# A gated feed-forward kernel on one core: first half of x first, DMA transposes for the second half, small first weight groups, warm-up matmuls and a split last tile

## The chip, the cores and the metric

The kernel runs on one core of a Trainium2 chip. The metric is device time in microseconds (us) of one execution. The kernel before takes 311.3 us (median of 12 runs, 311.04 to 311.73). The span of the profile is shorter than the device time: by 1.7 us in every run of the kernel before, by 1.9 to 2.2 us in every run of the changed kernel and its edits. So spans are compared with spans and times with times, and spans show about 0.35 us more of a gain than times do.

## The reference

```python
B, S, D, F = 32, 32, 1024, 3584          # 1024 tokens, bf16 everywhere
def reference(x, w_gate, w_up, w_down):
    return (gelu(x @ w_gate) * (x @ w_up)) @ w_down   # gelu: tanh approximation
```

In tiles of 128: 8 token tiles (`tt`), 8 chunks of D (`dc`), 28 chunks of F (`ft`). Matmuls take 512 tokens at a time, so there are two halves of the tokens (`th` = 0 and 1). Stage 1 has 28 x 2 = 56 "jobs" of 8 gate and 8 up matmuls. Stage 2 has 16 output pieces of 28 matmuls. That is 1,344 matmuls of 512 columns.

## The kernel before

Stage 1 needs x transposed (`xT`, with D on the partitions). The kernel loads all of x, transposes it on TensorE into PSUM, and VectorE copies it to SBUF. Only then does job 0 start.

```python
# SP: loads                                   (cut)
for (t0, t1) in x_chunks:                     # two DMAs of 1 MB
    sp.dma_start(out=x_nat[:, t0:t1, :], in_=x_v[:, t0:t1, :]).then_inc(sem_x, 16)
for fg in range(NFG):                         # 7 groups of 4 ft, 1 MB each, two buffers
    ... w_gate group, w_up group, then one chunk of w_down ...
for j2, (tt, dh) in enumerate(jobs2):         # stores: one row of tiles (256 KB) each
    if dh == DH - 1: ...

# TensorE                                     (cut)
pe.wait_ge(sem_x, 16 * NX)                    # ALL of x
for tt in range(TT):
    for dc in range(DT):
        ins = pe.transpose(...)               # 64 transposes
    ins.then_inc(sem_tp, 1)
pe.wait_ge(sem_xT, TT)                        # ALL copies
for j, (fg, ftl, th) in enumerate(jobs1):     # th is the fastest index
    ... 8 gate matmuls, 8 up matmuls ...
for j2, (tt, dh) in enumerate(jobs2):
    ... 28 matmuls of 512 columns ...

# VectorE: copies of xT, then the elementwise work of stage 1
# ScalarE: activations of stage 1, then all 16 evictions of stage 2
```

## Time and profile before

| | before |
|---|---|
| device time, median | 311.3 us |
| span of the profile | 310.0 us |
| TensorE busy | 294.9 us (95%) |
| first matmul of job 0 | 16.65 us |
| last eviction starts | 306.94 us |

The profile page's summary of the chain of work that ended last in the kernel before; shares of the span, by engine and by line:

```profile
PE 95%; DMA 3%; issue 1%; DVE 1%; ACT 0%; SPq 0%
PE ps L213 62%; PE ps L234 31%; DMA x_nat<-in_x_dram 3%; PE ps L193 2%; DVE xT L248 1%; ACT o_sb L310 0%; SPq L122 0%
```

L213 is stage 1 and L234 is stage 2, both on TensorE. The rest of the chain is the load of x, its transposes (L193) and its copies (L248), all at the start, and one eviction (L310) at the end. So time can come only from the two ends, or from shorter matmuls.

The timeline of the kernel before, its first 25 us. Columns: start in us, duration in us, engine, line, operation, output and inputs, count; in brackets the idle time before and what ended it. PE is TensorE and PEld its weight loads, DVE is VectorE, ACT is ScalarE, and SPq is SP, the engine that issues the DMAs. The traces hold 16 landing records for each DMA (32 for the two loads of x here); a load counts as landed at the last of them.

```profile
0.80 0.99 SPq L122 DMA_DIRECT2D x_nat<-in_x_dram  x2
...
9.39 6.20 PE L193 MATMUL ps<-ident,x_nat 128*128 128x128 bf16 x64 [9.39 <-DMA x_nat<-in_x_dram]
...
14.71 1.89 DVE L248 COPY xT<-ps 128x1024 bf16<-128x1024 bf16 x3 [0.16 <-PE ps L193]
16.65 1.41 PEld L213 LDWEIGHTS ps<-xT,wg_sb 128*128 128x128 bf16 x8 [1.23 <-DVE xT L248]
16.88 1.67 PE L213 MATMUL ps<-xT,wg_sb 128*128 128x512 bf16 x7 [1.28 <-DVE xT L248]
```

TensorE waits 9.4 us for x, transposes for 6.2 us, and waits for the last copy. The record of the very first matmul is missing (x7, not x8), so the first weight load, 16.65 us, is read as its start; the 1.28 us in the last line count to the second matmul. One transpose every 107 ns becomes one every 56 ns at 14.6 us: the clock of TensorE rose there. Below, "cold" is the slow pace and "warm" the fast one; for 512 columns they are 427 and 216 ns.

The timeline of the kernel before, its last us:

```profile
306.94 0.60 ACT L310 ACTIVATE o_sb<-ps 128x512 bf16<-128x512 f32 x1 [5.45 <-PE ps L234]
307.56 0.33 SPq L154 DMA_DIRECT2D out_dram<-o_sb  x1
```

The stores of the kernel before in its list of DMAs: count, size of one, median us from issue to landing.

```profile
out_dram<-o_sb SPq DMA_DIRECT2D x8, 256.0 KB, 2.0
```

After the last matmul come an eviction of 0.60 us, a store of 256 KB that lands 2.00 us after its issue, and 0.4 us to the end of the span.

### The profile page before, as it was taken

The numbers are of one execution on the slowest core, as the hardware profiler recorded it, in microseconds if no ns is written. First come the engines' busy times: TensorE is split into PE (matmuls) and PEld (weight loads), VectorE is DVE, ScalarE is ACT, GpSimd is POOL, SyncE is SP. The second block draws the span as 40 slices with busy tenths as digits, with TensorE's granted clock in tenths as the row PEclk, the third lists the DMA queues.
The fourth block names the chain that finished last, engine by engine and source line by source line (L and its number), as shares of the span: only waits on it lengthen the run. The fifth ranks groups of instructions, "written<-read, shape, count | busy, mean of one in ns | idle before, by whom it ended". The sixth has DMA issues, their size and how long they took to land.

```text
span 310.0 us, 3408 instructions
## 1 busy us (share of the span) xinstructions
PE 294.9 (95%) x1381; PEld 137.5 (44%) x1408; DVE 136.3 (44%) x120; ACT 102.1 (33%) x186; POOL 71.7 (23%) x62
## 2 busy tenths in 40 slices
PE   0789999999999999999999999999999999999995
PEld 0734444444444444444444444444444444444442
DVE  0534677667776777667766776674000000000000
ACT  1016544454445444554455445543000100100010
POOL 0003334333433343334333433343000000000000
PEclk9999999999999999999999999999999999999999
DMA  6990009005600910480097000000000000000000
GB/s 244 355 346 5 0 17 367 24 1 176 233 0 0 336 72 0 129 279 0 1 284 261 0 2 0 0 0 2 34 0 36 2 32 34 2 34 34 2 34 34
DMA packets 20479, 26.43 MB, mean 85 GB/s; under 512 B 496, under 2 KB 14832, under 8 KB 20464
## 3 DMA queue, kind: packets, MB, share of 16 engines
q1 hardware_dynamic: 20464, 26.22, 25.2%
q8 instruction: 11, 0.18, 0.2%
q14 instruction: 4, 0.03, 0.0%
HBM read 24.12 MB, written 2.10 MB: 85 GB/s over the span
## 4 chain that ended last, share of the span: by engine, by line
PE 95%; DMA 3%; issue 1%; DVE 1%; ACT 0%; SPq 0%
PE ps L213 62%; PE ps L234 31%; DMA x_nat<-in_x_dram 3%; PE ps L193 2%; DVE xT L248 1%; ACT o_sb L310 0%; SPq L122 0%
## 5 line engine op out<-in xcount | busy, mean ns | idle before, releaser
L213 PE MATMUL ps<-xT,wg_sb 128*128 128x512 bf16 x438 | 104.8, 379 | 1.8 <-DVE xT L248 1.3
L213 PE MATMUL ps<-xT,wu_sb 128*128 128x512 bf16 x440 | 105.1, 379 | 0.4
L178 POOL TENSOR_TENSOR hT<-gu_sb,s_sb 128x512 bf16<-128x512 f32 x56 | 71.0, 1267 | 143.4 <-ACT s_sb L294 143.4
L264 DVE SCALAR_TENSOR_TENSOR z_sb<-g_sb 128x512 f32<-128x512 f32 x56 | 97.1, 1733 | 0.0
L234 PE MATMUL ps<-wd_sb,hT 128*128 128x512 bf16 x439 | 96.4, 379 | 0.5
L282 ACT ACTIVATE g_sb<-ps 128x512 f32<-128x512 f32 x56 | 33.4, 597 | 119.1 <-PE ps L213 119.1
L259 DVE TENSOR_TENSOR gu_sb<-g_sb,ps 128x512 f32<-128x512 f32 x56 | 38.5, 688 | 66.2 <-ACT g_sb L285 66.2
L213 PEld LDWEIGHTS ps<-xT,wg_sb 128*128 128x128 bf16 x448 | 43.7, 98 | 53.9 <-DVE xT L248 1.2
L234 PEld LDWEIGHTS ps<-wd_sb,hT 128*128 128x128 bf16 x448 | 43.9, 98 | 52.8
L213 PEld LDWEIGHTS ps<-xT,wu_sb 128*128 128x128 bf16 x448 | 43.8, 98 | 52.9
L310 ACT ACTIVATE o_sb<-ps 128x512 bf16<-128x512 f32 x16 | 9.6, 597 | 83.6 <-PE ps L234 83.6
L294 ACT ACTIVATE s_sb<-z_sb 128x512 f32<-128x512 f32 x56 | 35.4, 632 | 1.9 <-DVE z_sb L264 1.9
L285 ACT ACTIVATE g_sb<-ps 128x512 f32<-128x512 f32 x56 | 33.1, 591 | 0.0
L193 PE MATMUL ps<-ident,x_nat 128*128 128x128 bf16 x64 | 6.2, 289 | 9.4 <-DMA x_nat<-in_x_dram 9.4
L248 DVE COPY xT<-ps 128x1024 bf16<-128x1024 bf16 x8 | 5.3, 689 | 11.2 <-PE ps L193 11.2
L193 PEld LDWEIGHTS ps<-ident,x_nat 128*128 128x128 bf16 x64 | 6.1, 135 | 9.4 <-issue 9.4
L282 ACT ACT_TABLE_LOAD x1 | 1.3, 1283 | 0.8 <-PEq L328 0.8
L294 ACT ACT_TABLE_LOAD x1 | 1.3, 1283 | 0.0
L165 POOL TENSOR_SCALAR_AFFINE_SELECT ident<-ones 128x128 bf16<-128x128 bf16 x1 | 0.3, 294 | 0.1
L163 POOL MEMSET ones<- 128x128 bf16 x1 | 0.2, 205 | 0.3 <-POOLq L328 0.3
L328 POOL MEMSET const-float32-0.0<- 128x1 f32 x1 | 0.1, 99 | 0.3 <-issue 0.3
L328 POOL MEMSET const-bfloat16-1.0<- 128x1 bf16 x1 | 0.1, 102 | 0.0
(2 smaller groups left out, 0.2 us busy)
## 6 DMA issues: line engine op xcount, KB each, us to landing
wg_sb<-in_w_gate_dram SPq DMA_DIRECT2D x7, 1024.0 KB, 6.7
wu_sb<-in_w_up_dram SPq DMA_DIRECT2D x7, 1024.0 KB, 9.3
wd_sb<-in_w_down_dram SPq DMA_DIRECT2D x7, 1024.0 KB, 11.3
x_nat<-in_x_dram SPq DMA_DIRECT2D x2, 1024.0 KB, 6.8
out_dram<-o_sb SPq DMA_DIRECT2D x8, 256.0 KB, 2.0
```

What stands on the lines that cost most here:

```text
L165: pool.affine_select(out=ident[:], in_=ones_sb[:], pattern=[[1, P]], compare_op=ALU.is_equal, fill=0.0, base=0, channel_multiplier=-1,).th ...
L178: pool.tensor_tensor(out=hT[:, ft, th * TW : (th + 1) * TW], in0=gu_sb[:, k, :], in1=s_sb[:, k, :], op=ALU.mult,).then_inc(sem_h, 1)
L193: ins = pe.transpose(out=bank_bf[:, dc * P : (dc + 1) * P], in_=x_nat[:, tt, dc * P : (dc + 1) * P], identity=ident[:],)
L213: last = pe.matmul(bank, lhsT=wsb[:, slot, dc, ftl * P : (ftl + 1) * P], rhs=xT[:, dc, th * TW : (th + 1) * TW], start=(dc == 0), stop=(dc ...
L234: last = pe.matmul(bank, lhsT=hT[:, fc, tt * P : (tt + 1) * P], rhs=wd_sb[:, fc, dh * DW : (dh + 1) * DW], start=(fc == 0), stop=(fc == FT ...
L248: dve.tensor_copy(out=xT[:, :, tt * P : (tt + 1) * P], in_=bank_bf[:, 0 : DT * P].rearrange("p (dc t) -> p dc t", dc=DT),).then_inc(sem_xT, 1)
L259: dve.tensor_tensor(out=gu_sb[:, k, :], in0=g_sb[:, k, :], in1=bu, op=ALU.mult).then_inc(sem_d1, 1)
L264: dve.scalar_tensor_tensor(out=z_sb[:, k, :], in0=g2_sb[:, k, :], scalar=GELU_A, in1=g_sb[:, k, :], op0=ALU.add, op1=ALU.mult,).then_inc(s ...
L282: act.activation(out=g_sb[:, k, :], in_=bg, func=ACT.Copy).then_inc(sem_a1, 1)
L285: act.activation(out=g2_sb[:, k, :], in_=bg, func=ACT.Square).then_inc(sem_a1, 1)
L294: act.activation(out=s_sb[:, k, :], in_=z_sb[:, k, :], func=ACT.Sigmoid, scale=GELU_C2).then_inc(sem_a2, 1)
L310: act.activation(out=o_sb[:, ob, dh * DW : (dh + 1) * DW], in_=ps[:, s2, 0:DW], func=ACT.Copy,).then_inc(sem_o, 1)
```

## The change

Its intent is to start stage 1 sooner and end sooner:

1. Only the first half of x (two DMAs of 512 KB) is loaded and transposed on TensorE. The second half goes from HBM straight into `xT` by eight DMA transposes, issued behind the first three weight groups.
2. The first jobs are reordered, so that 7 jobs need only the first half of the tokens.
3. The first two weight groups hold 2 x 128 columns (512 KB per matrix), the others 3 x 128, in three buffers.
4. Six warm-up matmuls run before the transposes and four after, to raise TensorE's clock (it rose at 7.6 us in the profile after, at 14.6 in that before).
5. ScalarE and VectorE take turns at stage 2's evictions, stores are per piece (128 KB), and the last 512 columns become 256 + 128 + 128.

```diff
-    FG = 4 ...            NBUF_W = 2
+    FGMAX = 3
+    NBUF_W = 3
+    for s0 in (2, 2): ...                     # first two groups
+    NWARM = 6
...
+        if groups[0][1] == 2 and TH == 2:     # jobs 0-6: th 0, jobs 7-13: th 1
+            for th in range(2):
+                jobs1 += [(g, f, th) for g in range(3) for f in range(groups[g][1])]
...
+                if tt == TT - 1 and dh == DH - 1 and DW % 128 == 0 and DW > 256:
+                    jobs2.append((tt, dh * DW, DW - 256))
+                    jobs2.append((tt, dh * DW + DW - 256, 128))
+                    jobs2.append((tt, dh * DW + DW - 128, 128))
...
+            for c in range(NXC0):             # first half of x only
+                x_load(c)
+            w_load(sp, 0) ...
+                if g == 2:
+                    for dc in range(DT):
+                        sp.dma_start_transpose(
+                            xT[:, dc, TT_SPLIT * P : N], xf[TT_SPLIT * P : N, dc * P : (dc + 1) * P]
+                        ).then_inc(sem_xtr, 16)
...
-            pe.wait_ge(sem_x, 16 * NX)
-            for tt in range(TT):
+            warm(NWARM)
+            for tt in range(TT_SPLIT):        # 4 of 8; each waits for its own chunk of x
+                transposes(tt)
+            warm(4)
...
+                if j == 7:
+                    pe.wait_ge(sem_xtr, 16 * DT)
...
+            for j2, (tt, cs, ncol) in enumerate(jobs2):   # VectorE: odd pieces
+                dve.tensor_copy(...)
```

## The prediction

> **What bounds the kernel now.** TensorE. The chain of waits gives PE 95% of the 310.0 us span, the load of x 3%, the x^T copies on VectorE 1%. In the timeline the 1,344 matmuls of 512 columns run from 16.65 to 306.9 us without a gap, one every 0.216 us. Nothing in the change shortens that stream, so only the head (16.65 us) and the tail (3.1 us) can give time back.
>
> **Head, before.** PE idles until all 2 MB of x have landed (9.3 us; the first MB at 6.35), does 64 transposes, 48 at 107 ns and the last at 56 ns (the clock rose at about 14.6 us), until 15.6, and waits 1.3 us for the last copy.
>
> **Head, after.** By the landing times of before: 0.5 MB of x at about 4.9 us, 1 MB at 6.35. Packets of 2 KB moved at about 390 GB/s and of 1 KB at 349; from these I estimate 287 GB/s for the new 512-byte rows: w_gate of group 0 at about 8.2 us, w_up at 10.0. PE: six warm-up matmuls from 2.0 to 4.6 us; 16 transposes to about 6.6; 16 more to 7.8 (warm) or 8.3; four more warm-ups hide in the 1.3 us that the last copy takes. First matmul at about 9.3 us (8.7 to 10.1), clock warm. Gain: 7.3 us.[...] PE is nearly always busy from 2 us.[...]
>
> **Second half of x^T.** Eight DMA transposes of 128 KB replace 32 PE transposes and four copies. Behind 4.7 MB of loads they start at about 16 to 18.5 us. Job 7 needs all, at 9.3 + 7 x 3.454 = 33.5 us: about 15 us for 1 MB, so 70 GB/s are enough.[...] I expect no stall, but this is the largest risk: below 70 GB/s PE stalls microsecond for microsecond.
>
> **Steady state.** Three buffers of smaller groups and the reordered first jobs: all loads stay ahead, no change. Stage 2's evictions were off the chain.
>
> **Tail.** The last 512 columns become 256 + 128 + 128: 28 x (0.110 + 2 x 0.056) against 28 x 0.216 is +0.17 us (56 ns is the pitch of the warm transposes, which load new weights too). The last eviction falls from 0.60 to about 0.2 us; the output's landing stays at 2.0. Net -0.2 us.
>
> **Sum.** 311.5 - 7.3 - 0.2 = 304.0 us, 2.4% less, near the 2% line (305.3). Range 302.7 to 307.5. Chances: faster 0.74, within 2% 0.20, slower 0.06.
>
> **What would show it.** First 512-column gate matmul at 9.3 us in the timeline; pitch 0.216 with no gap at job 7 (about 33 us); no DMA-to-xT entry among PE's waits; 128-column matmuls at 56 ns at the end; about 2.3 us from the last eviction to the end.
>
> **What would make it wrong.** DMA transposes slow or late, so that PE idles before job 7; w_up of group 0 later than 11 us because 512-byte rows are slower than estimated; a cold clock at the first matmuls (each then costs 0.21 us more); group 2 late (needed at 23 us).

## The result

The changed kernel takes 303.5 us (median of 8 runs, 303.34 to 304.42), against 311.3 us. The ratio is 0.9754 (95% interval 0.9744 to 0.9765). Ratios are the mean time of one kernel's fast runs over that of the other's of the same rounds, so not quite the ratio of the medians. All outputs are correct.

The page's summary of the chain after:

```profile
PE 96%; DMA 2%; issue 1%; SPq 0%; DVE 0%
PE ps L310 64%; PE ps L336 32%; DMA wg_sb<-in_w_gate_dram 2%; SPq L198 0%; DVE x_nat L379 0%
```

The load at the head of the chain is now that of w_gate, not of x. The timeline after, its first 45 us:

```profile
1.90 2.74 PE L267 MATMUL ps<-warm,ident 128*128 128x512 bf16 x6 [1.90 <-POOL ident L239]
...
4.43 3.48 PE L281 MATMUL ps<-ident,x_nat 128*128 128x128 bf16 x32
...
7.23 1.41 DVE L350 COPY xT<-ps 128x1024 bf16<-128x1024 bf16 x2 [0.16 <-PE ps L281]
...
9.06 1.41 PEld L310 LDWEIGHTS ps<-xT,wg_sb 128*128 128x128 bf16 x8 [0.78 <-DMA wg_sb<-in_w_gate_dram]
9.07 1.68 PE L310 MATMUL ps<-xT,wg_sb 128*128 128x512 bf16 x7 [0.29 <-DMA wg_sb<-in_w_gate_dram]
...
12.19 13.59 SPq L214 DMA_TRANSPOSE xT<-in_x_dram  x8
...
33.25 1.89 PE L310 MATMUL ps<-xT,wg_sb 128*128 128x512 bf16 x8
```

The first matmul starts at 9.07 us. The copies of xT ended at 8.64 (7.23 + 1.41); what TensorE waited for was w_gate, whose last piece landed at 9.02 us by the trace's landing records. Job 7, the first to need the second half of x^T, starts at 33.25 us with no bracket: no wait. The last DMA transpose had landed at 27.22 us, which leaves a margin of 6.0 us.

The timeline after, its last us:

```profile
295.73 3.73 PE L336 MATMUL ps<-wd_sb,hT 128*128 128x256 bf16 x60
...
299.50 0.29 DVE L379 CAST x_nat<-ps 128x128 bf16<-128x128 f32 x1 [2.70 <-PE ps L336]
```

The last two stores after, in the list of DMAs (the buffer is that of x):

```profile
out_dram<-x_nat SPq DMA_DIRECT2D x2, 32.0 KB, 1.5
```

The last eviction takes 0.29 us, and the last store, 32 KB, lands 1.48 us after its issue. The 256-column matmuls follow each other every 109 ns and the 128-column ones every 56 ns.

Where the 8.3 us of the span went (310.0 to 301.7):

| part | before | after | difference |
|---|---|---|---|
| start to first matmul | 16.65 | 9.07 | -7.58 |
| first matmul to start of the last eviction | 290.29 | 290.43 | +0.14 |
| start of the last eviction to end | 3.07 | 2.20 | -0.87 |

Stage 1 and stage 2 themselves did not change: 1,344 x 0.216 us is 290.3.

### The profile page after: what moved, and what is told of

The parts are those of the page before. It is cut to its first block, busy times and chain, and to the rows that moved or that the text cites. A ratio compares the mean times of both kernels' runs of the same rounds, so it can differ in the third digit from the quotient of the medians.

```text
span 301.7 us, 3497 instructions
## 1 busy us (share of the span) xinstructions
PE 295.8 (98%) x1415; PEld 139.0 (46%) x1442; DVE 139.3 (46%) x125; ACT 97.6 (32%) x179; POOL 72.2 (24%) x63
## 4 chain that ended last, share of the span: by engine, by line
PE 96%; DMA 2%; issue 1%; SPq 0%; DVE 0%
PE ps L310 64%; PE ps L336 32%; DMA wg_sb<-in_w_gate_dram 2%; SPq L198 0%; DVE x_nat L379 0%
## 5 line engine op out<-in xcount | busy, mean ns | idle before, releaser
L336 PE MATMUL ps<-wd_sb,hT 128*128 128x512 bf16 (+2 forms) x495 | 96.5, 355 | 0.5
L336 PEld LDWEIGHTS ps<-wd_sb,hT 128*128 128x128 bf16 x504 | 47.0, 98 | 50.1
L379 DVE CAST x_nat<-ps 128x512 bf16<-128x512 f32 (+2 forms) x9 | 5.6, 618 | 88.1 <-PE ps L336 76.7
L419 ACT ACTIVATE x_nat<-ps 128x512 bf16<-128x512 f32 (+1 forms) x9 | 5.1, 562 | 86.3 <-PE ps L336 86.3
L267 PE MATMUL ps<-warm,ident 128*128 128x512 bf16 x10 | 3.8, 528 | 1.9 <-POOL ident L239 1.9
L350 DVE COPY xT<-ps 128x1024 bf16<-128x1024 bf16 x4 | 2.8, 692 | 5.9 <-PE ps L281 5.8
L281 PEld LDWEIGHTS ps<-ident,x_nat 128*128 128x128 bf16 x32 | 3.4, 144 | 0.6 <-DMA x_nat<-in_x_dram 0.5
L281 PE MATMUL ps<-ident,x_nat 128*128 128x128 bf16 x32 | 3.5, 304 | 0.0
L267 PEld LDWEIGHTS ps<-warm,ident 128*128 128x128 bf16 x10 | 1.1, 120 | 3.2 <-POOL ident L239 1.9
```

Of the source, the lines that this page charges most:

```text
L267: ins = pe.matmul(ps[:, 7, :], lhsT=ident[:], rhs=warm_sb[:], start=True, stop=True)
L281: ins = pe.transpose(out=bank_bf[:, dc * P : (dc + 1) * P], in_=x_nat[:, tt, dc * P : (dc + 1) * P], identity=ident[:],)
L336: last = pe.matmul(bank, lhsT=hT[:, fc, tt * P : (tt + 1) * P], rhs=wd_sb[:, fc, cs : cs + ncol], start=(fc == 0), stop=(fc == FT - 1),)
L379: dve.tensor_copy(out=o_sb[:, tt, cs : cs + ncol], in_=ps[:, s2, 0:ncol]).then_inc(sem_od, 1)
L419: act.activation(out=o_sb[:, tt, cs : cs + ncol], in_=ps[:, s2, 0:ncol], func=ACT.Copy,).then_inc(sem_oa, 1)
```

## The experiments

Each is an edit of the changed kernel, in three groups of runs, each group on one chip. All outputs were correct. The changed kernel itself was run again in the third group (0.9734, interval 0.9721 to 0.9747; median 303.22 us). The same kernel thus differs by 0.2% between groups, and differences of under about 0.6 us between groups are not read as effects.

| run | what | median us | ratio to before (95%) |
|---|---|---|---|
| (the change) | | 303.5 | 0.9754 (0.9744-0.9765) |
| e1_no_warm | no warm-ups | 305.83, two groups | 0.9798 (0.9769-0.9827) |
| e2_x_all_pe | all of x by TensorE | 307.04 | 0.9854 (0.9841-0.9867) |
| e3_interleaved | job order of before | 319.3 | 1.0248 (1.0233-1.0263) |
| e4_tail_whole | last piece unsplit | 303.7 | 0.9752 (0.9739-0.9765) |
| e5_wide_tr | 4 wide DMA transposes | 303.37 | 0.9756 (0.9736-0.9776) |
| e6_double_tr | 16 DMA transposes | 307.47 | 0.9894 (0.9857-0.9931) |
| e7_groups_of_4 | weight groups of before | 305.5 | 0.9823 (0.9798-0.9848) |
| e8_early | attempt at a shorter head | 303.34 | 0.9742 (0.9728-0.9755) |
| e9_no_warm_b | e1, one look | 306.02 | |
| e10_only_early6 | without the late four | 302.87 | 0.9731 (0.9718-0.9744) |
| e11_only_late4 | without the early six | 304.05 | 0.9761 (0.9748-0.9774) |
| e12_change_again | the change | 303.22 | 0.9734 (0.9721-0.9747) |

### The second half of x out of the way: e2

```diff
-        TT_SPLIT = (TT // 2 // XC) * XC if TT >= 2 else TT
+        TT_SPLIT = TT
@@ SP: the DMA transposes are taken out
@@ TensorE
-            warm(4)
-                if j == 7:
-                    pe.wait_ge(sem_xtr, 16 * DT)
```

> The change with no DMA transpose: all 2 MB of x are loaded first and transposed on TensorE in 64 transposes, and the four later warm-ups are left out. Theory: the DMA transposes gain by taking 1 MB of x out of the queue ahead of group 0, so w_gate lands about 2.8 us later and the first gate matmul is at about 11.9 us: 306.3 us, with everything after it the same. Rival (the halved work on TensorE is what gains): the first matmul stays near 9 to 10 us and only 0.5 to 1 us are lost.

Measured: 307.04 us, 3.5 us longer than the change, all of it in the head. The timeline of e2:

```profile
10.43 1.07 PE L276 MATMUL ps<-ident,x_nat 128*128 128x128 bf16 x16 [0.33 <-DMA x_nat<-in_x_dram]
...
12.49 1.42 PEld L302 LDWEIGHTS ps<-xT,wg_sb 128*128 128x128 bf16 x8 [1.17 <-DMA wg_sb<-in_w_gate_dram]
12.52 1.67 PE L302 MATMUL ps<-xT,wg_sb 128*128 128x512 bf16 x7 [1.03 <-DVE xT L342]
```

The first matmul is at 12.5 us. The w_gate of group 0 landed at 12.19 us (9.02 after), as the theory has it. But the chain of x was as late: its last chunk landed at 10.38 us, and VectorE's copies ended at 12.38. So the expectation is right in size (3.5 for 2.8 us), and half right in mechanism: 1 MB more of x in front of the queue delays both w_gate and x^T, to within 0.2 us of each other. The rival, that the halved work on TensorE is what gains, expected at most 1 us.

e2 also shows what the split of x does not explain. Its first matmul is still 4.1 us earlier than in the kernel before (12.52 against 16.65), though its x landed 1.1 us later (10.38 against 9.26). By then 48 of its 64 transposes were done, chunk by chunk, and the last 16 ran warm; the kernel before starts all 64 only when all of x is there. So of the 7.6 us of the head about 3.5 belong to the split and about 4.1 to the waits by chunk, the warm clock and the smaller first group together. No run takes these three apart.

### The job order: e3

```diff
-        if groups[0][1] == 2 and TH == 2:
-            for th in range(2):
-                jobs1 += [(g, f, th) for g in range(3) for f in range(groups[g][1])]
-            g_start = 3
-        else:
-            g_start = 0
+        g_start = 0
-                if j == 7:
+                if j == 1:
                     pe.wait_ge(sem_xtr, 16 * DT)
```

> The change with the job order of before (the two halves of the tokens alternate), so that job 1 needs the second half of x^T. Theory: job 0 runs at 9.1 us as after, job 1 waits for the last DMA transpose, which landed at 27.2 us, where it would have started at 12.5: 14.7 us lost, and 1.5 to 3.5 us more because the clock falls while TensorE waits: 320 us (318 to 322). The reordering is then what hides the DMA transposes. Rival (the transposes are slow in the profile after only because nobody waits for them): under 8 us lost.

Measured: 319.3 us, slower than the kernel before. The timeline of TensorE in e3:

```profile
11.66 1.89 PE L305 MATMUL ps<-xT,wu_sb 128*128 128x512 bf16 x8
27.30 3.60 PE L305 MATMUL ps<-xT,wg_sb 128*128 128x512 bf16 x8 [13.75 <-DMA xT<-in_x_dram]
30.69 2.27 PE L305 MATMUL ps<-xT,wu_sb 128*128 128x512 bf16 x8
```

Job 1 waited 13.7 us, until 27.30, just behind the last landing at 27.25. Eight matmuls then took 3.60 us where eight warm ones take 1.89: the clock was low until 31.5 us, 4.2 us at half speed, which is 2.1 us lost; the 1.5 to 3.5 expected were the author's estimate, which no run before e3 had shown. The span of this profile is 16.8 us longer than that after: 13.7 and 2.1, and 0.85 because its first matmul came at 9.92 us. By the medians 15.8 us are lost; the profiled run, 320.57 us, is the slowest of the four. The reordering of seven jobs is what makes a slow second half of x^T free.

### How slow the DMA transposes are, and the margin: e5 and e6

The eight DMA transposes landed at 21.23, 21.71, 22.22, 22.74, 23.36, 24.45, 25.80 and 27.22 us in the profile after. The first four had queued up behind the weights and follow each other every 0.50 us: 128 KB in 0.50 us is about 260 GB/s. The last four come every 1.1 to 1.4 us; their issues on SP take 1.26 us each and start every 1.30 us.

```diff
@@ e5
-                    for dc in range(DT):
+                    for dc in range(0, DT, 2):
                         sp.dma_start_transpose(
-                            xT[:, dc, TT_SPLIT * P : N], xf[TT_SPLIT * P : N, dc * P : (dc + 1) * P]
+                            xT[:, dc : dc + 2, TT_SPLIT * P : N],
+                            xf[TT_SPLIT * P : N, dc * P : (dc + 2) * P],
                         ).then_inc(sem_xtr, 16)
-                    pe.wait_ge(sem_xtr, 16 * DT)
+                    pe.wait_ge(sem_xtr, 16 * (DT // 2))
@@ e6
+                    for dc in range(DT):      # the same again, into a part of x_nat that nobody reads
+                        c0 = (dc % 2) * (N - TT_SPLIT * P)
+                        sp.dma_start_transpose(
+                            x_nat[:, TT_SPLIT + dc // 2, c0 : c0 + N - TT_SPLIT * P],
+                            xf[TT_SPLIT * P : N, dc * P : (dc + 1) * P],
+                        ).then_inc(sem_xtr, 16)
-                    pe.wait_ge(sem_xtr, 16 * DT)
+                    pe.wait_ge(sem_xtr, 16 * 2 * DT)
```

> The change with four DMA transposes of 512 x 256 instead of eight of 512 x 128. The last four of the eight were issued one every 1.30 us and landed one every 1.1 to 1.4 us. If that time belongs to each instruction, four take half of it and the last lands at about 23 us instead of 27.2; if it belongs to each element (or each small tile), each takes about 2.5 us and the last lands at about 27 us as before. The total time is the same either way (303.5 us, within 0.3), as no one waits for them.

Measured for e5: 303.37 us, no change in time. The records of the tile xT in e5, beside those of the change; the three durations are the shortest, median and longest issue in ns. First the change, then e5:

```profile
L214 SPq DMA_TRANSPOSE xT<-in_x_dram x8: 1261/1262/3542, 12.2 to 24.5; - x8
```

```profile
L214 SPq DMA_TRANSPOSE xT<-in_x_dram x4: 1304/2147/3812, 12.3 to 20.6; - x4
```

An issue of twice the data takes 1,304 ns at the shortest against 1,261. So the time belongs to the instruction, not to the elements; this rests on one issue, as the other three took 2.0 to 3.8 us. The four landed at 21.02, 21.84, 22.93 and 24.02 us; the last at 24.0 instead of 27.2 (expected: about 23). Their spacing, 1.09 us for 256 KB at the end, is 240 GB/s.

> The change with each DMA transpose issued twice, the second time into a part of the x buffer that nobody reads; job 7 waits for all 16. Theory: eight more at 1.30 us each land at about 27.2 + 10.4 = 37.6 us, while job 7 was due at 33.3 us: TensorE stalls 4.3 us there and the time is 307.8 us (307 to 309.5, the upper end if the clock falls). This shows the margin of the change, about 6 us. Rival[...]: the second eight take 4 us, end at 31 us, and nothing is lost.

Measured for e6: 307.47 us (306.70 to 309.87), 4.0 us longer than the change. The records of the second eight in e6, and then TensorE's waits:

```profile
L219 SPq DMA_TRANSPOSE x_nat<-in_x_dram x8: 1261/1262/1270, 24.5 to 33.7; - x8
```

```profile
PE ps L316 <- DMA x_nat<-in_x_dram: 3.3, 1, 3.3
```

All eight issues take 1.26 us. The last landing came at 36.21 us (the first issue was at 11.2 us, 1 us earlier than in the profile after, which explains most of the distance to the 37.6 expected), and job 7 waited 3.3 us for it. Two of the four times are those of the profile (306.70 and 306.74); the other two, 308.21 and 309.87, have no profile and stay open. The rival, 4 us for eight at the 0.50 us of those that queue up, is refuted. With e3 this shows that the margin is real: eight more transposes cost less than their 10.4 us only because about 6 us were free.

### The small first groups: e7

```diff
-    FGMAX = 3
-    NBUF_W = 3
+    FGMAX = 4
+    NBUF_W = 2
-    for s0 in (2, 2):
+    for s0 in ():
@@ the jobs of the first two groups are reordered: 8 of th 0, then 8 of th 1
@@ SP: the DMA transposes and one chunk of w_down follow the first two groups
```

> The change with the weight groups of before: seven groups of 4 x 128 columns in two buffers, rows of 1 KB, with the split of x, the reordered jobs (8 + 8 over the first two groups), the warm-ups and the new tail kept. Theory: 1 MB of w_gate after 1 MB of x lands at about 9.0 to 9.4 us (1 KB rows at 350 GB/s make up for twice the bytes), w_up at 12.2 where it is needed at 11.0: the small first groups are worth about 1.3 us: 304.9 us. Rival (the small groups are what makes the head short): over 3 us lost.

Measured: 305.5 us (304.72 to 307.30), 2.0 us longer by the medians. The timeline of e7:

```profile
9.19 1.90 PE L311 MATMUL ps<-xT,wg_sb 128*128 128x512 bf16 x8 [0.29 <-DMA wg_sb<-in_w_gate_dram]
...
12.20 1.41 PEld L311 LDWEIGHTS ps<-xT,wu_sb 128*128 128x128 bf16 x8 [1.60 <-DMA wu_sb<-in_w_up_dram]
```

The gate matmuls start at 9.19 us, as expected: 1 MB in rows of 1 KB had landed at 9.15 us, hardly later than 0.5 MB in rows of 512 bytes (9.02 in the profile after). The up matmuls then start at 12.2 us instead of 10.9: 1.3 us, the size predicted. This run's profile is 1.4 us longer than that after; the timed runs lost 0.6 us more, and their spread leaves that open.

### The warm-ups: e1, e9, e10, e11 and e12

```diff
@@ e1 and e9: both; e10: only the second; e11: only the first
-            warm(NWARM)
@@
-            warm(4)
```

> The change without its ten warm-up matmuls. Theory (the head is set by when group 0 of w_gate lands, and the warm-ups matter only through the clock): the first gate matmul stays near 9.1 us;[...] 0 to 2 us are lost, about 0.8 us in the mean: 304.3 us, transposes all at 107 ns. Rival (the warm-ups carry a large part of the gain): over 2 us longer. Second rival (they carry nothing, since the cold transposes alone raise the clock in time): within 0.2 us of the change.

Measured for e1: 303.44, 303.58, 305.76, 305.90, 306.00 and 306.19 us. The median of that, 305.8, is no typical time: there are two groups, 2.4 us apart. The expectation, 0 to 2 us lost and 0.8 in the mean, was too low: four of six lost 2.3 to 2.7. The profile fell in the fast group, so e9 looked again.

> The kernel of e1 once more, for a profile: its six times fell into two groups, two of 303.5 us and four of 305.8 to 306.2, and the profile was of the fast group. Theory[...]: without warm-ups TensorE is busy from 4.4 to 7.7 us, rests 1.2 us and is busy again[...]. In a run of 306 us the profile shows cold matmuls up to about 13.7 us (4.8 us cold cost 2.4 us). Rival: the slow group has a late landing of group 0, and no cold matmuls.

Measured for e9: 306.02 us, of the slow group. The timelines of TensorE in e1 (fast group) and in e9 (slow group):

```profile
4.46 3.57 PE L280 MATMUL ps<-ident,x_nat 128*128 128x128 bf16 x32 [4.46 <-DMA x_nat<-in_x_dram]
8.91 1.89 PE L308 MATMUL ps<-xT,wg_sb 128*128 128x512 bf16 x8 [0.88 <-DVE xT L348]
```

```profile
4.45 3.57 PE L280 MATMUL ps<-ident,x_nat 128*128 128x128 bf16 x32 [4.45 <-DMA x_nat<-in_x_dram]
9.11 3.60 PE L308 MATMUL ps<-xT,wg_sb 128*128 128x512 bf16 x8 [1.08 <-DMA wg_sb<-in_w_gate_dram]
12.49 2.46 PE L308 MATMUL ps<-xT,wu_sb 128*128 128x512 bf16 x8
```

The same work, at nearly the same start, takes 3.60 us for eight matmuls in e9 and 1.89 in e1. In e9 the clock rose at 13.7 us, 4.6 us after the first matmul; 4.6 us at half speed lose 2.3 us, which is the distance of the two groups. The clock is read from the pace of the matmuls: the profile's own record of the granted clock stays at 1.00 from 9 to 13 us of e9, where 512 columns take 427 ns, and shows 0.50 at the same pace in e3. The rival, a late landing, is refuted: w_gate landed at 9.06 us. So the warm-ups are worth 2.4 us in some runs and nothing in others. How long the clock takes to rise was not shown before these runs: the losses expected for e1, e10 and e11 and the cold stretch expected for e9 were the author's estimates.

> The change with the six warm-ups before the transposes and without the four after them. Theory: TensorE is busy from 1.9 to 7.7 us[...], so most times are those of the change, and perhaps one in four is longer by up to 2 us: median 303.5 us. Rival (the four late ones are what bridges the gap): the two groups of e1 again.

> The change with the four warm-ups after the transposes and without the six before them. Theory: TensorE is busy from 4.4 us on with gaps of under half a us[...]: 0 to 1.1 us lost, median 303.9 us, none at 306. Rival (only an early start helps): the two groups of e1 again.

> The changed kernel itself, for a comparison on the same chip with the two above and for the spread of its times: 303.3 to 304.4 us, most near 303.5; where a run is near 304.4, w_gate of group 0 lands after 9.5 us or the first matmuls are cold.

Measured: e10 302.79 to 303.49 us, e11 303.41 to 304.25, e12 302.83 to 303.49, all on one chip. No run of either kind is near 306. The early six alone do as well as all ten (0.9731 and 0.9734). The late four alone lose 0.8 us by the medians, inside the range expected. By the times of four runs each, either set kept the clock from staying low far into the matmuls; without both, five of seven runs (e1 and e9) were slow. No run of e12 was near 304.4, so the cause of the two such runs of the change was not caught and stays open.

### The tail: e4

```diff
-                if tt == TT - 1 and dh == DH - 1 and DW % 128 == 0 and DW > 256:
+                if False:
```

> The change with the last 512 columns in one piece. Theory: the stream of matmuls gets 0.17 us shorter, the last eviction goes from 0.29 to 0.69 us and its output's landing from 1.5 to 1.7 us: 0.4 us longer, 303.9 us. Rival (the tail's 0.9 us come from the smaller output transfers and the second evicting engine alone): within 0.1 us, or shorter.

Measured: 303.7 us, ratio 0.9752: no difference to the change that the times can show. The timeline of e4 at its end:

```profile
298.70 0.69 DVE L379 CAST x_nat<-ps 128x512 bf16<-128x512 f32 x1 [11.39 <-PE ps L336]
```

From there to the end of the span (301.5) it is 2.8 us, against 2.2 with the split. From the first matmul to the end of the span, which leaves the head out, it is 293.2 us in e4 and 292.6 to 292.7 in seven profiles with the split tail (after, e1, e2, e5, e8, e10, e12). So the split is worth about 0.5 us in the records, near the 0.4 expected. In the time it drowns: this profile's first matmul came at 8.34 us, 0.7 us earlier than in the profile after, for no reason that the edit gives. The kernel before takes 293.4 us from its first matmul to the end. So of the 0.73 us that tail and stream gain together, about 0.5 belong to the split and, by subtraction, 0.2 to the smaller store and the other engine; that last part was not tried by itself.

### An attempt to do better: e8

```diff
@@ w_gate of group 0 in two DMAs (dc 0-3, dc 4-7), each with its own semaphore
+                        if j == 0 and wsb is wg_sb and dc == DT // 2:
+                            pe.wait_ge(sem_wg0b, 16)
@@ warm-ups: from a tile that VectorE fills, without waiting for the identity
-                        ps[:, 7, :], lhsT=ident[:], rhs=warm_sb[:], start=True, stop=True
+                        ps[:, 7, :], lhsT=warm_sb[:, 0:P], rhs=warm_sb[:], start=True, stop=True
-            warm(NWARM)
+            warm(8)
```

> An attempt to beat the change: w_gate of group 0 in two DMAs of four chunks each, so that the first four matmuls wait for half of it, and eight warm-ups that start at about 1.2 us because they use a tile that VectorE fills, not the identity. Theory: the first half lands at about 8.0 us, so the first matmul waits for x^T instead, at 8.7 us[...]: 0.3 to 1.0 us gained, 303.0 us. Rival (the slowest DMA engine, not the amount of data, sets the landing): nothing gained.

Measured: 303.34 us, ratio 0.9742: not told apart from the change. The timeline of e8:

```profile
4.91 3.10 PE L290 MATMUL ps<-ident,x_nat 128*128 128x128 bf16 x32
...
6.86 2.03 DVE L362 COPY xT<-ps 128x1024 bf16<-128x1024 bf16 x3 [0.16 <-PE ps L290]
...
9.03 1.89 PE L321 MATMUL ps<-xT,wg_sb 128*128 128x512 bf16 x8 [0.16 <-DVE xT L362]
```

The halves of w_gate landed at 6.59 and 7.50 us, so here the wait for w_gate is gone. That the two DMAs did it is not shown: in e10 the undivided load landed at 7.50 us too. But the copies of x^T end at 8.89 us and bound the start instead. Eight warm-ups were too many: they hold up the transposes until 4.91 us, though x had landed at 4.26. The two chains that meet at the first matmul are about equally long. None of the runs here is a version that clearly beats the change.

### What varies from run to run

In the profiles of the change and of the edits that leave the head alone, group 0's w_gate landed anywhere from 7.50 (e10) to 9.88 us (e3). The first of the 16 engines always landed between 6.9 and 7.3 us; the slowest made the difference. Why some engines lag, no run here shows. When the clock rises varies as well: at 4.6 us in the profile of e12 and at 7.6 in that after, which are one kernel, and the copies of x^T ended at 7.62 and 8.64. In these profiles the first matmul came between 8.16 (e10) and 9.92 us (e3), and effects of that size are hidden.

## Why the prediction was right

The prediction was 304.0 us; measured were 303.5. Point by point:

- **Bound: right.** Only the two ends moved; the stream from the first matmul to the last eviction grew by 0.14 us (predicted: 0.17).
- **First matmul at 9.3 us: right in size (9.07), wrong in what bounds it, and so in part luck.** The prediction had w_gate at 8.2 us and x^T last, at 9.1 us or later. In the profile x^T was ready at 8.64 and w_gate landed last, at 9.02. Two errors in the 8.2 worked against each other: the 1.05 MB of x landed at 5.51 us, not at 6.35, and the slowest engine landed w_gate 2.1 us after the first. The rate was near the estimate of 287: by the packet records the loads from 1.05 to 2.10 MB ran at 285 GB/s (1.05 MB in 3.68 us). In e10, where the 16 engines landed within 0.2 us, w_gate was there at 7.50.
- **Clock warm at the first matmul: right.** It rose at 7.6 us, while the transposes ran. That this is worth up to 2.4 us, and that it depends on the run, the prediction named only as a risk; e1 and e9 measured it.
- **DMA transposes: no stall, right; the time that they take, wrong.** They took 10 us, from their first packet at 17.1 to 27.2. The author's estimate was shorter, at a rate that no run had shown. Where the transposes queue up, one lands every 0.50 us (128 KB, about 260 GB/s), which would be 4.0 us for eight; but SP needs 1.26 us to issue each, and the prediction had no term for that. The 16 us from their first packet to job 7 (33.25 us) hid the error; e6 shows it at work when the slack is used up, and e3 when there is none.
- **Tail, "net -0.2 us": right in sign, too small.** Measured is -0.87 us at the end and +0.14 in the stream. The mis-sized term is the landing of the last store, taken as unchanged at 2.0 us: 32 KB landed in 1.48 us. The eviction fell to 0.29 us, not 0.2.
- **Steady state unchanged: right.** The profile after shows no wait of TensorE beyond the head.

The errors of -0.3 us (head: -7.58 for -7.3) and -0.5 us (tail and stream: -0.73 for -0.2) have the same sign and make up the difference between 8.3 us in the span and the 7.5 predicted. In device time the two profiled runs differ by 8.0 us (311.74 and 303.75) and the medians by 7.8: of what the span gained, 0.35 us went to the time outside it (1.7 us before, 2.05 after), which no trace shows. The close hit on 304.0 owes something to that too.

## What to carry to other kernels

When one engine is busy from its first instruction of real work to its last, count the bytes that stand in the queue ahead of that first instruction, and move out of the way what is needed later (1 MB cost 3.5 us in e2); reorder the work until the late part has slack (here seven jobs, 24 us), because the slow transposes cost nothing under slack (6.0 us of margin in the profile after) and 15.8 us without it (e3). Take a DMA's cost apart into issue, rate and landing: four DMA transposes of 512 x 256 had landed at 24.02 us (e5), eight of 512 x 128 at 27.22 (after). Warm-up matmuls are an insurance: look at the single times, since a median hides two groups of 303.5 and 306 us (e1).

## What the traces show of the clock and the DMAs

- The clock rose during transposes: in the trace before, TensorE had done nothing but transposes since 9.39 us when their pitch went from 107 to 56 ns at 14.6 us. In e1 too only transposes had run when the first matmuls of 512 columns started warm at 8.91 us; in e9, after the same transposes, they started cold at 9.11 us. These are transposes issued as here (`pe.transpose`); the records call them MATMUL.
- The moment of the rise varies: in the runs with the early six warm-ups the clock rose from 2.7 (e12, 4.61 us) to 6 us (e7, about 8 us) after the first of them, at 1.89 us.
- DMA transposes that queue up land one every 0.50 us (128 KB, about 260 GB/s, in the profile after). SP takes 1.26 us to issue one of 512 x 128 and took 1.30 us for the quickest of 512 x 256 (e5), so that eight of 128 KB in a row, one every 1.30 us (e6), run at about 100 GB/s.
- Loads in rows of 512 bytes ran at 285 GB/s (in the profile after, 1.05 MB in 3.68 us), of 1 KB at 349 and of 2 KB at about 390 (both in the profile before).
- The 16 landings of the first w_gate load lay within 0.2 us (e10) to 3.0 us (e3) of each other, and the cause is open.
